# First block's second product from whole float32 words; w_out split in two afterwards

## The chip, the cores and the metric

The kernel runs on one core of one Trainium2 chip. The metric is the device time of one execution in microseconds (us). The kernel before takes 892.45 us (median of 3 runs, 891.19 to 892.52).

## What is computed

Three layers follow one another on 3072 tokens (4 sequences of 768) of width 384: a gated linear attention with decay (8 heads of 48), a dense gated feed-forward layer, and a mixture of 8 experts of which one is taken for each token. The change lies in the second layer:

```python
def _moe_ref(x, w_gate, w_val, w_out, rms_g):
    rms = np.sqrt(np.mean(x * x, axis=-1, keepdims=True) + 1e-06)
    xn = x / rms * rms_g
    g = xn @ w_gate
    silu = g * (1.0 / (1.0 + np.exp(-g)))
    val = xn @ w_val
    return (silu * val @ w_out).astype(np.float32)
```

`w_gate` and `w_val` are 384 x 1536, `w_out` is 1536 x 384. The experts' routing logits (16 columns) are linear in this layer's output, so the kernel appends `w_out @ w_gates` to `w_out` as 16 further columns: the second product is 400 wide.

## The kernel before, in words

**Number format.** The weights of the second layer arrive in HBM as float64. `decode` turns a piece of them into float32 on the chip: a DMA brings 64-bit words into `raw`, ScalarE scales the low words (L113), VectorE shifts and merges the high words (L114, L118), GpSimd adds both (L122) into a float32 tile `dt`. TensorE's one-pass format `fp32r` holds fewer bits than float32, so every operand is kept as two fp32r parts, high and low: ScalarE writes the high part (L125) and VectorE the rest by subtraction (L129). A product of two such operands is three matmuls: high by high, high by low, low by high (`mm3`, and L547 to L549 for the second product).

**Blocks.** The second layer runs over eight blocks of 384 tokens (`for j in range(NB)`), each over twelve slices f of the hidden width. `l1(f)` forms the two first products into two PSUM banks `a` (18 fp32r matmuls each 384 wide for both), ScalarE applies silu to the first (L531), VectorE multiplies by the second (L533), giving `sil`; ScalarE makes its high part `hh` (L535) and VectorE its low part `hl` (L538). `l2(f)`, two slices later, multiplies the 3 x 128 token columns of `hh` and `hl` as stationary operand by the two parts `wo[f // 2]` of `w_out`, adding into three PSUM banks `l` over all f (nine matmuls, 400 wide). At the end of a block ScalarE copies the banks to `xr` (L906).

**The first block** carries more work than the others. The 18 pieces of weights (for every two f two pieces of `w_gate` and `w_val` and one of `w_out`) are decoded while it runs: `decode_step` starts a piece's stages and finishes those of earlier pieces, six steps ahead of the block (`START`), the rest at every second `slot()` inside it. `route_columns` forms the 16 further columns for each f: TensorE transposes the decoded `w_out` rows (L505), ScalarE copies them to `wt` (L509), three small float32 matmuls follow (L513), and the result is split into the parts in `wo` (L516, L517). And in the slots of every block the attention of the next block's three tiles is computed, with float32 matmuls on TensorE (L408, L414, L431, L444, L450, L466), products on VectorE and GpSimd, a row norm `ss` (ACT L458, POOL L459 and L460), the scaling of `y` (ACT L480), its transposition (PE L484) and the two parts `xh`, `xl` (ACT L488, DVE L491).

**Order.** Each engine runs its instructions in the order in which the code is written (`tc.manual_schedule`), so a late instruction holds up all that stand behind it on the same engine. Tiles rotate in pools: `dt` has three buffers, the ring has 12 small and 6 big slots, and `wo` takes big ones.

Of the kernel before, what the change touches and what calls it, by code (L numbers as in the profile page):

```python
# [9 lines left out]
F32 = mybir.dt.float32  # L10
FR = mybir.dt.float32r
BF16 = mybir.dt.bfloat16
I32 = mybir.dt.int32
U32 = mybir.dt.uint32
AF = mybir.ActivationFunctionType
ALU = mybir.AluOpType
# [6 lines left out]
def kernel(  # L23
# [20 lines left out]
    nc = tc.nc  # L44
    B, S, _, H, D = rkv.shape
    N, DM = out.shape
    DFF = w_gate.shape[1]
    E, _, F2 = w1.shape
    P = 128
# [3 lines left out]
    KD = DM // P  # L53
    KF = DFF // P
# [4 lines left out]
    WIDTH = DM + 2 * E  # L59
# [17 lines left out]
    ring = ctx.enter_context(tc.tile_pool(name="ring", bufs=12))  # L77
# [20 lines left out]
    def words(src):  # L98
        return src.bitcast(U32) if src.dtype != U32 else src

    def decode(n, loads, dst, more=None):

        raw = loaded(n)
        for put, words_in in loads:
            nc.sync.dma_start(out=put(raw), in_=words_in)
        yield  # L110
        t = dec.tile([P, 2, DM], U32, tag="dt", bufs=3, name="dt")
        ti, tf, low = t.bitcast(I32), t.bitcast(F32), raw.bitcast(I32)[:, :, :, 0]
        nc.scalar.activation(out=low, in_=raw[:, :, :, 0], func=AF.Copy, scale=2.0 ** -29)  # L113
        nc.vector.tensor_scalar(  # L114
            t, raw[:, :, :, 1], 3, 0x3FFFFFF8, op0=ALU.logical_shift_left, op1=ALU.bitwise_and
        )
        yield
        nc.vector.scalar_tensor_tensor(  # L118
            out=t, in0=raw[:, :, :, 1], scalar=0xC0000000, in1=t, op0=ALU.bitwise_and,
            op1=ALU.bitwise_or,  # L120
        )
        nc.gpsimd.tensor_tensor(out=ti, in0=ti, in1=low, op=ALU.add)  # L122
        yield
        hi, lo = dst()
        nc.scalar.activation(out=hi, in_=tf, func=AF.Copy)  # L125
        if more:
            more(tf)
        yield
        nc.vector.tensor_tensor(out=lo, in0=tf, in1=hi.bitcast(F32), op=ALU.subtract)  # L129
        yield  # L130

    def split(raw, dst):
        nc.scalar.activation(out=dst[:, 0], in_=raw, func=AF.Copy)
        nc.vector.tensor_tensor(out=dst[:, 1], in0=raw, in1=dst[:, 0].bitcast(F32), op=ALU.subtract)
# [33 lines left out]
    def ring_view(shape, dtype=F32, big=None):  # L168
        n = 1
        for x in shape:  # L170
            n *= x
        t = slot_of(n, dtype, "rv", big)
        names = "abc"[:len(shape)]
        dims = " ".join(names)
        return t.rearrange(f"p ({dims}) -> p {dims}", **dict(zip(names[1:], shape[1:])))
# [87 lines left out]
    p1 = ph1.enter_context(tc.tile_pool(name="p1", bufs=1))  # L263
# [232 lines left out]

    gv = {}
    wo = {}
    routed = {}

    def route_columns(f, tf):

        o = bank("m", 3, [P, KD, P])
        for kk in range(KD):
            nc.tensor.transpose(o[:, kk], tf[:, kk * P:(kk + 1) * P], c["ident"])  # L505

        wt = turned[:, f % 4] if f < KF - 2 else dec.tile([P, 2, DM], F32, tag="dt", bufs=3, name="wt")[:, 0]
        wt = wt.rearrange("p (c f) -> p c f", c=KD)
        nc.scalar.activation(out=wt, in_=o, func=AF.Copy)  # L509
        yield  # L510
        o = bank("m", 3, [P, 2 * E])
        for kk in range(KD):
            nc.tensor.matmul(o, wt[:, kk], c["wr"][:, kk], start=kk == 0, stop=kk == KD - 1)  # L513
        t = wo[f // 2]
        hi, lo = t[:, 0, f % 2, DM:WIDTH], t[:, 1, f % 2, DM:WIDTH]
        nc.scalar.activation(out=hi, in_=o, func=AF.Copy)  # L516
        nc.vector.tensor_tensor(out=lo, in0=o, in1=hi.bitcast(F32), op=ALU.subtract)  # L517
        yield

    def l1(f, xh, xl, n, sub):  # L520
        t = gv[f]
        pg = []
        for a in range(2):
            o = bank("a", 2, [P, n])
            for kk in range(KD):
                mm3(o, t[:, 0, a, kk], t[:, 1, a, kk], xh[:, kk, 0:n], xl[:, kk, 0:n],
                    kk == 0, kk == KD - 1)
            pg.append(o)
            if a == 0:
                sil = p2.tile([P, n], F32, tag="sil", name="sil")  # L530
                nc.scalar.activation(out=sil, in_=o, func=AF.Silu)  # L531
                sub()
        nc.vector.tensor_tensor(out=sil, in0=pg[1], in1=sil, op=ALU.mult)  # L533
        hh = p3.tile([P, n], FR, tag="hh", name="hh")
        nc.scalar.activation(out=hh, in_=sil, func=AF.Copy)  # L535
        sub()
        hl = p3.tile([P, n], FR, tag="hl", name="hl")
        nc.vector.tensor_tensor(out=hl, in0=sil, in1=hh.bitcast(F32), op=ALU.subtract)  # L538
        return hh, hl

    def l2(f, h, acc):
        hh, hl = h
        t = wo[f // 2]
        wh, wl = t[:, 0, f % 2], t[:, 1, f % 2]
        for j, o in enumerate(acc):
            sl = slice(j * P, (j + 1) * P)
            nc.tensor.matmul(o, hh[:, sl], wh, start=f == 0, stop=False)  # L547
            nc.tensor.matmul(o, hh[:, sl], wl, start=False, stop=False)  # L548
            nc.tensor.matmul(o, hl[:, sl], wh, start=False, stop=f == KF - 1)  # L549
# [98 lines left out]
    def exhaust(g):  # L648
        for _ in g:
            pass  # L650

    with tc.manual_schedule():
# [34 lines left out]
        for f in range(KF):  # L687
            def dst(f=f):
                gv[f] = ring.tile([P, 2, 2, KD, P], FR, tag="ring", name="gv")
                return tuple(gv[f][:, s].rearrange("p a c f -> p a (c f)") for s in range(2))  # L690
            pieces.append(([
                (lambda t, a=a: t[:, a].rearrange("p (c f) t -> p c (f t)", c=KD),
                 src[:, 2 * f * P:2 * (f + 1) * P].rearrange("(c p) f -> p c f", p=P))
                for a, src in enumerate((words(w_gate), words(w_val)))
            ], dst))
            if f % 2:
                def dst(f=f):
                    wo[f // 2] = ring.tile(
                        [P, 2, 2, WIDTH], FR, tag="big", bufs=6, name="wo"
                    )  # L700
                    return tuple(wo[f // 2][:, s, :, 0:DM] for s in range(2))

                def more(tf, f=f):
                    for i in range(2):
                        routed[f - 1 + i] = route_columns(f - 1 + i, tf[:, i])

                pieces.append(([
                    (lambda t: t.rearrange("p a n t -> p a (n t)"),
                     words(w_out)[(f - 1) * P:(f + 1) * P, :].rearrange("(a p) n -> p a n", p=P))
                ], dst, more))  # L710
        gens_w = []
        done_w = [0]

# [32 lines left out]
        def decode_step():  # L746
            n = done_w[0]
            if n < len(pieces) + LAG:
                advance(n + 2, 1)
                advance(n, 2)  # L750
                if n >= LAG:
                    advance(n - LAG, 5)
                advance(n, 3)
                if n >= LAG - 1:
                    advance(n - LAG + 1, 4)
                done_w[0] += 1
            else:
                done_w[0] += 1
            routed_step()

        def weights_to(i):
# [72 lines left out]
        for j in range(NB):  # L834
# [24 lines left out]
            for f in range(KF + 2):  # L859
                if f < KF:  # L860
                    if j == 0:
                        weights_to(f + f // 2 + 1)
                    hs[f] = l1(f, xs[0], xs[1], n, slot)
                if f >= 2:
                    if f - 2 in routed:
                        exhaust(routed.pop(f - 2))
                    l2(f - 2, hs.pop(f - 2), acc)
                    slot()
                if j == NB - 1:
                    if f == 3:  # L870
                        lead = pick(c)
                        xw = expert_weights(0, lead)
                    if f >= 4:
                        next(xw, None)
                    if f == KF - 3:
                        xg0 = ring_view([EARLY // P, ROW])
                        nc.sync.dma_start(
                            out=xg0,
                            in_=scr.rearrange("(e a) c -> e a c", e=E)[ds(lead, 1), 0:EARLY, :]
                            .rearrange("o (t p) c -> p (o t) c", p=P),  # L880
                        )
                    if f == KF:
                        x0 = ring_view([2, KD, EARLY], FR)
                        transpose_in(c, xg0, EARLY, x0[:, 0], x0[:, 1])
                if j == 1 and ini < E:
                    init_rows(c, ini)
                    ini += 1
# [412 lines left out]
```

## Time and profile before

| what | value |
|---|---|
| median of 3 runs | 892.45 us |
| the profiled execution | 890.04 us |
| its span, first to last instruction | 888.3 us |
| TensorE busy (PE) | 853.3 us, 96% |
| VectorE busy (DVE) | 523.3 us, 59% |
| ScalarE busy (ACT) | 316.7 us, 36% |
| GpSimd busy (POOL) | 208.8 us, 24% |
| first block, first matmul to end | 44.05 to 152.3 us |
| second block, to its copy of the banks | 152.3 to 224 us |

The profiled execution is 1.7 us longer than its span and lies 2.4 us below the median of the runs. The records of the matmuls overlap, since a matmul's time from start to end is longer than the distance to the next one; the price of a matmul in a row of matmuls is therefore the distance between two starts, not its own length.

### The profile page before, as it was taken

The numbers are of one execution on the slowest core, as the hardware profiler recorded it, in microseconds if no ns is written. First come the engines' busy times: TensorE is split into PE (matmuls) and PEld (weight loads), VectorE is DVE, ScalarE is ACT, GpSimd is POOL, SyncE is SP. The second block draws the span as 40 slices with busy tenths as digits, with TensorE's granted clock in tenths as the row PEclk, the third lists the DMA queues.
The fourth block names the chain that finished last, engine by engine and source line by source line (L and its number), as shares of the span: only waits on it lengthen the run. The fifth ranks groups of instructions, "written<-read, shape, count | busy, mean of one in ns | idle before, by whom it ended". The sixth has DMA issues, their size and how long they took to land. (4 is left out here: it accounts for less than half of the span.)

```text
span 888.3 us, 15961 instructions
## 1 busy us (share of the span) xinstructions
PE 853.3 (96%) x6220; PEld 808.4 (91%) x6220; DVE 523.3 (59%) x1052; ACT 316.7 (36%) x667; POOL 208.8 (24%) x282
## 2 busy tenths in 40 slices
PE   7778989999999999999999999999999999999994
PEld 4577889999999999999999999999998999999994
DVE  8898854665565556465376366343556565565651
ACT  4655443232322322322323323223444434443531
POOL 6644431223131032032132132010011021122111
PEclk8889979999999999999999999999999999999998
DMA  8753421663221122042023020012164445445510
GB/s 231 207 178 107 134 89 48 165 170 117 73 63 55 46 81 55 12 122 55 10 82 80 29 81 20 1 53 83 58 199 150 132 148 153 145 124 176 167 40 22
DMA packets 63728, 87.98 MB, mean 99 GB/s; under 512 B 5538, under 2 KB 55220, under 8 KB 63652
## 3 DMA queue, kind: packets, MB, share of 16 engines
q1 hardware_dynamic: 60014, 77.36, 30.0%
q0 software_dynamic: 3312, 9.56, 2.9%
q8 instruction: 49, 0.80, 0.4%
q14 instruction: 27, 0.22, 0.1%
q10 hardware_dynamic: 326, 0.03, 0.0%
HBM read 70.71 MB, written 16.58 MB: 98 GB/s over the span
## 5 line engine op out<-in xcount | busy, mean ns | idle before, releaser
L164 PE MATMUL a<-xh,gv 128*128 128x384 f32 x1152 | 326.7, 349 | 1.6 <-ACT xh L488 1.5
L164 PEld LDWEIGHTS a<-xh,gv 128*128 128x128 f32 x1152 | 215.3, 193 | 4.8 <-ACT xh L488 1.6
L164 PE MATMUL a<-xl,gv 128*128 128x384 f32 x576 | 197.2, 342 | 0.2 <-DVE xl L491 0.2
L533 DVE TENSOR_TENSOR sil<-a,sil 128x384 f32<-128x384 f32 x96 | 53.3, 555 | 115.9 <-PE a L164 115.6
L164 PEld LDWEIGHTS a<-xl,gv 128*128 128x128 f32 x576 | 111.0, 193 | 0.6 <-DVE xl L491 0.6
L535 ACT ACTIVATE hh<-sil 128x384 fp32r<-128x384 f32 x96 | 50.5, 526 | 167.6 <-DVE sil L533 162.5
L531 ACT ACTIVATE sil<-a 128x384 f32<-128x384 f32 x96 | 47.3, 492 | 169.3 <-PE a L164 163.8
L164 PE MATMUL a<-xh,w1s 128*128 128x272 f32 (+7 forms) x384 | 106.1, 337 | 0.4 <-DVE hl L972 0.4
L547 PE MATMUL l<-wo,hh 128*128 128x400 f32 x288 | 102.3, 355 | 0.0
L548 PE MATMUL l<-wo,hh 128*128 128x400 f32 x288 | 99.6, 346 | 0.0
L549 PE MATMUL l<-wo,hl 128*128 128x400 f32 x288 | 98.9, 343 | 0.0
L240 POOL DMA_INDIRECT out_dram<-row,iu x30 | 35.4, 1181 | 196.3 <-DVE row L983 152.5
L164 PE MATMUL l<-hh,rows 128*128 128x272 f32 (+5 forms) x288 | 80.1, 342 | 0.0
L972 DVE SCALAR_TENSOR_TENSOR hl<-a,hh 128x256 fp32r<-128x256 f32 (+8 forms) x72 | 38.6, 539 | 67.5 <-ACT hh L971 67.4
L538 DVE TENSOR_TENSOR hl<-sil,hh 128x384 fp32r<-128x384 f32 x96 | 57.0, 594 | 35.6 <-ACT hh L535 35.6
L164 PEld LDWEIGHTS a<-xh,w1s 128*128 128x128 f32 x384 | 69.8, 188 | 1.6 <-DVE hl L972 0.6
L971 ACT ACTIVATE hh<-a 128x256 fp32r<-128x256 f32 (+8 forms) x72 | 34.6, 480 | 93.1 <-PE a L164 92.4
L164 PE MATMUL a<-xl,w1s 128*128 128x272 f32 (+7 forms) x192 | 64.5, 336 | 0.0
L398 POOL TENSOR_TENSOR y<-vt,g 128x384 f32<-128x384 f32 x23 | 22.4, 975 | 167.5 <-issue 62.6
L547 PEld LDWEIGHTS l<-wo,hh 128*128 128x128 f32 x288 | 54.3, 189 | 1.2
L549 PEld LDWEIGHTS l<-wo,hl 128*128 128x128 f32 x288 | 54.6, 190 | 0.2
L548 PEld LDWEIGHTS l<-wo,hh 128*128 128x128 f32 x288 | 54.2, 188 | 0.0
(235 smaller groups left out, 1394.1 us busy)
## 6 DMA issues: line engine op xcount, KB each, us to landing
raw<-in_moe_w_dram SPq DMA_DIRECT2D x64, 384.0 KB, 3.3
set<-in_feat_dram SPq DMA_DIRECT2D x46, 192.0 KB, 4.0
rk<-in_rkv_dram SPq DMA_DIRECT2D x18, 384.0 KB, 4.6
scr<-zrow SPq DMA_DIRECT2D x8, 788.0 KB, 6.2
set<-in_feat_dram SPq DMA_DIRECT2D x46, 96.0 KB, 2.4
vt<-in_rkv_dram SPq DMA_DIRECT2D x23, 192.0 KB, 2.4
raw<-in_moe_w_gate_dram SPq DMA_DIRECT2D x8, 384.0 KB, 3.8
raw<-in_moe_w_val_dram SPq DMA_DIRECT2D x8, 384.0 KB, 3.9
```

The costliest lines, as they stand in the source:

```text
L164: nc.tensor.matmul(o, a, b, start=start and i == 0, stop=stop and i == 2, skip_group_check=True)
L240: ins = nc.gpsimd.indirect_dma_start(out=dst, out_offset=bass.IndirectOffsetOnAxis(ap=idx, axis=0), in_=rows, in_offset=None, bounds_check ...
L398: nc.gpsimd.tensor_tensor(out=y, in0=vv, in1=g.unsqueeze(2).to_broadcast([P, H, D]), op=ALU.mult)
L531: nc.scalar.activation(out=sil, in_=o, func=AF.Silu)
L533: nc.vector.tensor_tensor(out=sil, in0=pg[1], in1=sil, op=ALU.mult)
L535: nc.scalar.activation(out=hh, in_=sil, func=AF.Copy)
L538: nc.vector.tensor_tensor(out=hl, in0=sil, in1=hh.bitcast(F32), op=ALU.subtract)
L547: nc.tensor.matmul(o, hh[:, sl], wh, start=f == 0, stop=False)
L548: nc.tensor.matmul(o, hh[:, sl], wl, start=False, stop=False)
L549: nc.tensor.matmul(o, hl[:, sl], wh, start=False, stop=f == KF - 1)
L971: nc.scalar.activation(out=hh, in_=o, func=AF.Relu)
L972: nc.vector.scalar_tensor_tensor(out=hl, in0=o, scalar=0.0, in1=hh.bitcast(F32), op0=ALU.max, op1=ALU.subtract)
```

## The change

In block 0 alone the second product is formed from float32 operands. `l1` ends with the product `h` as one float32 tile, without `hh` and `hl`; `l2_whole` runs one float32 matmul for each 128 tokens in place of three fp32r ones. `decode` leaves a piece of `w_out` as float32 in `whole_w`, two pieces in one big slot of the ring (the last in a tile of its own), and `route_columns` writes its 16 columns there whole. The two parts `wo` that the seven later blocks use are made by `split_wo`, once for each piece, from the whole words: in the `decode_step`s that come after the last piece, or when `l2` of block 1 needs them. `dt` has two buffers instead of three, and `wt` a tile in the pool where `hl` stands.

```diff
@@ def decode(n, loads, dst, whole=None):
-        t = dec.tile([P, 2, DM], U32, tag="dt", bufs=3, name="dt")
+        if whole:
+            t = whole().bitcast(U32)
+        else:
+            t = dec.tile([P, 2, DM], U32, tag="dt", bufs=2, name="dt")
...
+        if whole:
+            dst(tf)
+            yield
+            yield
+            return
         hi, lo = dst()
         nc.scalar.activation(out=hi, in_=tf, func=AF.Copy)
...
@@ def route_columns(f, tf):
-        wt = turned[:, f % 4] if f < KF - 2 else dec.tile([P, 2, DM], F32, tag="dt", bufs=3, name="wt")[:, 0]
+        wt = p3.tile([P, DM], F32, tag="hl", name="wt").rearrange("p (c f) -> p c f", c=KD)
...
-        nc.scalar.activation(out=hi, in_=o, func=AF.Copy)
-        nc.vector.tensor_tensor(out=lo, in0=o, in1=hi.bitcast(F32), op=ALU.subtract)
+        nc.scalar.activation(out=whole_w[f // 2][:, f % 2, DM:WIDTH], in_=o, func=AF.Copy)
+    def split_wo(k):
+        for f in (2 * k, 2 * k + 1):
+            if f in routed:
+                exhaust(routed.pop(f))
+        wo[k] = ring.tile([P, 2, 2, WIDTH], FR, tag="big", bufs=6, name="wo")
+        split(whole_w[k].rearrange("p a n -> p (a n)"), wo[k].rearrange("p s a n -> p s (a n)"))
@@ def l1(f, xh, xl, n, sub, whole=False):
+        if whole:
+            h = p3.tile([P, n], F32, tag="hh", name="h")
+            nc.vector.tensor_tensor(out=h, in0=pg[1], in1=sil, op=ALU.mult)
+            sub()
+            return h
+    def l2_whole(f, h, acc):
+        w = whole_w[f // 2][:, f % 2]
+        for j, o in enumerate(acc):
+            nc.tensor.matmul(
+                o, h[:, j * P:(j + 1) * P], w, start=f == 0, stop=f == KF - 1,
+                skip_group_check=True,
+            )
@@ def decode_step():
-            else:
-                done_w[0] += 1
+            elif len(wo) < KF // 2:
+                split_wo(len(wo))
+            done_w[0] += 1
@@ for j in range(NB): ... for f in range(KF + 2):
-                    hs[f] = l1(f, xs[0], xs[1], n, slot)
+                    hs[f] = l1(f, xs[0], xs[1], n, slot, j == 0)
...
-                    l2(f - 2, hs.pop(f - 2), acc)
+                    if j == 0:
+                        l2_whole(f - 2, hs.pop(f - 2), acc)
+                    else:
+                        while len(wo) <= (f - 2) // 2:
+                            split_wo(len(wo))
+                        l2(f - 2, hs.pop(f - 2), acc)
```

On ScalarE, in the middle of the first block, around the scaling of a tile's `y`, before:

```order
L113 ACTIVATE rv<-rv 128x768
L125 ACTIVATE gv<-dt 128x768
L516 ACTIVATE wo<-m 128x16
L535 ACTIVATE hh<-sil 128x384
L476 ACTIVATE states<-m 48x4x48 x2
L480 ACTIVATE y<-y,ss 128x384
L488 ACTIVATE xh<-m,g_col 128x128 x3
```

and of the change, at the same place (lines are six to eleven higher; `rv` in the third row is the slot with the whole words):

```order
L116 ACTIVATE rv<-rv 128x768
L133 ACTIVATE gv<-dt 128x768
L520 ACTIVATE rv<-m 128x16
L482 ACTIVATE states<-m 48x4x48 x2
L486 ACTIVATE y<-y,ss 128x384
L494 ACTIVATE xh<-m,g_col 128x128 x3
```

The instruction `hh`, which reads VectorE's `sil`, no longer stands ahead of `y`.

On VectorE, a little earlier in the program, from the preparation of `kq` to the addition that completes the same tile's `y` and the next piece, before:

```order
L376 RECIPROCAL front<-kq 128x4
L377 TENSOR_TENSOR kq<-set_81,kq 128x4x128
L114 TENSOR_SCALAR dt<-raw_673 128x768
L129 TENSOR_TENSOR wo<-dt,wo 128x2x384
L118 SCALAR_TENSOR_TENSOR dt<-raw_673,dt 128x768
L538 TENSOR_TENSOR hl<-sil,hh 128x384
L454 TENSOR_TENSOR y<-m,y 128x384
```

and of the change:

```order
L382 RECIPROCAL front<-kq 128x4
L383 TENSOR_TENSOR kq<-set_81,kq 128x4x128
L117 TENSOR_SCALAR dt<-raw_662 128x768
L121 SCALAR_TENSOR_TENSOR dt<-raw_662,dt 128x768
L460 TENSOR_TENSOR y<-m,y 128x384
```

The low parts of `w_out` and of `h` are gone from between them.

On VectorE at the end of the first block, around the last two products, before:

```order
L533 TENSOR_TENSOR sil<-a,sil 128x384
L472 TENSOR_TENSOR states<-m,states 48x4x48 x2
L538 TENSOR_TENSOR hl<-sil,hh 128x384
L491 SCALAR_TENSOR_TENSOR xl<-m,g_col,xh 128x128 x3
L517 TENSOR_TENSOR wo<-m,wo 128x16
L533 TENSOR_TENSOR sil<-a,sil 128x384
L538 TENSOR_TENSOR hl<-sil,hh 128x384
```

and of the change, with one row more ahead of them:

```order
L140 TENSOR_TENSOR wo<-rv,wo 128x800
L546 TENSOR_TENSOR h<-a,sil 128x384
L478 TENSOR_TENSOR states<-m,states 48x4x48 x2
L497 SCALAR_TENSOR_TENSOR xl<-m,g_col,xh 128x128 x3
L140 TENSOR_TENSOR wo<-rv,wo 128x800
L546 TENSOR_TENSOR h<-a,sil 128x384
L140 TENSOR_TENSOR wo<-rv,wo 128x800 x2
```

Four of the six splits stand here; the other two follow in the first slices of block 1. SyncE's and GpSimd's instructions keep their order.

## Rows read from the trace of the kernel before

**Rows 1.** Page, busy time, share of the span and instructions of an engine.

```profile
PE 853.3 (96%) x6220; PEld 808.4 (91%) x6220; DVE 523.3 (59%) x1052; ACT 316.7 (36%) x667; POOL 208.8 (24%) x282
```

**Rows 2.** Stretches: length; busy PE, PEld, DVE, ACT, POOL; granted clock; DMA share; GB/s.

```profile
44.00:121.00 77.00, 65.38 (x457) 61.79 (x458) 65.76 (x94) 39.40 (x80) 34.60 (x22) 0.88 0.45 141
121.00:152.30 31.30, 30.17 (x229) 28.68 (x228) 14.21 (x32) 8.89 (x23) 4.67 (x9) 0.91 0.10 27
152.30:224.00 71.70, 71.70 (x593) 68.42 (x592) 43.56 (x90) 21.04 (x49) 19.56 (x34) 1.00 0.53 151
```

**Rows 3.** Waits of TensorE in the first block: total us, times, longest.

```profile
PE m L484 <- ACT y L480: 5.6, 2, 3.7
PE m L505 <- POOL dt L122: 5.3, 3, 2.3
...
PE m L414 <- ACT wt L509: 1.1, 1, 1.1
PE m L431 <- DVE rq L387: 0.4, 1, 0.4
```

**Rows 4.** Same view as rows 2, three stretches at the lower clock.

```profile
85.70:92.50 6.80, 6.80 (x26) 6.80 (x27) 3.20 (x8) 3.37 (x8) 1.83 (x1) 0.50 0.00 1
...
116.50:123.20 6.70, 6.70 (x25) 6.70 (x24) 3.07 (x6) 3.09 (x7) 3.42 (x2) 0.50 0.27 106
...
130.10:133.40 3.30, 3.30 (x15) 2.86 (x15) 2.49 (x4) 0.02 (x1) 1.43 (x1) 0.50 0.69 179
```

**Rows 5.** Timeline of TensorE: start, length; nine matmuls of one l2, block 1.

```profile
201.06 0.34 PE L547 MATMUL l<-wo,hh 128*128 128x400 f32 x1
...
202.71 0.18 PE L557 MATMUL m<-acc,one_b 128*128 128x8 bf16 x1
```

**Rows 6.** Timeline of TensorE, float32 matmuls of the attention, 96 columns wide.

```profile
107.60 0.30 PE L444 MATMUL m<-states,rq 128*64 128x96 f32 x1
...
107.60 0.30 PE L444 MATMUL m<-states,rq 128*64 128x96 f32 x2
...
108.03 0.35 PE L444 MATMUL m<-states,rq 128*64 128x96 f32 x4
108.21 0.39 PE L450 MATMUL m<-vt,am 128*64 128x48 f32 x8
```

**Rows 7.** Groups on VectorE in the first block: busy us, mean ns, idle before.

```profile
L538 DVE TENSOR_TENSOR hl<-sil,hh 128x384 fp32r<-128x384 f32 x12 | 10.3, 859 | 3.6 <-ACT hh L535 3.6
...
L129 DVE TENSOR_TENSOR wo<-dt,wo 128x768 fp32r<-128x768 f32 x5 | 5.8, 1166 | 0.0
...
L517 DVE TENSOR_TENSOR wo<-m,wo 128x16 fp32r<-128x16 f32 x12 | 2.0, 167 | 5.8 <-ACT wo L516 5.8
```

**Rows 8.** The same of ScalarE.

```profile
L125 ACT ACTIVATE gv<-dt 128x768 fp32r<-128x768 f32 x9 | 7.6, 840 | 5.3 <-PE m L513 5.3
L535 ACT ACTIVATE hh<-sil 128x384 fp32r<-128x384 f32 x12 | 6.3, 525 | 24.8 <-DVE sil L533 24.8
```

**Rows 9.** Timelines, start and length: ACT, POOL and PE around the longest wait.

```profile
83.85 0.52 ACT L535 ACTIVATE hh<-sil 128x384 fp32r<-128x384 f32 x1 [1.75 <-DVE sil L533]
...
81.67 1.14 POOL L460 TENSOR_TENSOR ss<-ss,mhalf 128x1 f32<-128x1 f32 x1
...
85.62 0.88 PE L484 MATMUL m<-ident,y 128*128 128x128 f32 x3 [3.73 <-ACT y L480]
```

**Rows 10.** Timelines around waits for dt; then all hl (ns, min/median/max).

```profile
59.62 1.87 POOL L122 TENSOR_TENSOR dt<-dt,rv 128x768 int32<-128x768 int32 x1 [2.85 <-issue]
...
60.46 1.45 DVE L538 TENSOR_TENSOR hl<-sil,hh 128x384 fp32r<-128x384 f32 x1 [0.59 <-ACT hh L535]
...
61.53 0.85 ACT L125 ACTIVATE gv<-dt 128x768 fp32r<-128x768 f32 x1
...
105.56 0.55 PE L505 MATMUL m<-ident,dt 128*128 128x128 f32 x3 [1.10 <-POOL dt L122]
...
L538 DVE TENSOR_TENSOR hl<-sil,hh x96: 544/558/1734, 55.5 to 631.9; 128x384 fp32r<-128x384 f32 x96
```

More of the change, by code (lines that the diff above doesn't have):

```diff
@@ L99, in words, with decode @@
         return src.bitcast(U32) if src.dtype != U32 else src
-    def decode(n, loads, dst, more=None):
+    def decode(n, loads, dst, whole=None):
         raw = loaded(n)
@@ L123, in decode @@
         yield
+        if whole:
[3 more added lines that the diff above has]
+            return
         hi, lo = dst()
         nc.scalar.activation(out=hi, in_=tf, func=AF.Copy)
-        if more:
-            more(tf)
         yield
@@ L498 @@
     wo = {}
+    whole_w = {}
     routed = {}
@@ L505, in route_columns @@
             nc.tensor.transpose(o[:, kk], tf[:, kk * P:(kk + 1) * P], c["ident"])
-        wt = turned[:, f % 4] if f < KF - 2 else dec.tile([P, 2, DM], F32, tag="dt", bufs=3, name="wt")[:, 0]
-        wt = wt.rearrange("p (c f) -> p c f", c=KD)
+        wt = p3.tile([P, DM], F32, tag="hl", name="wt").rearrange("p (c f) -> p c f", c=KD)
         nc.scalar.activation(out=wt, in_=o, func=AF.Copy)
@@ L513, in route_columns, with l1 @@
             nc.tensor.matmul(o, wt[:, kk], c["wr"][:, kk], start=kk == 0, stop=kk == KD - 1)
-        t = wo[f // 2]
-        hi, lo = t[:, 0, f % 2, DM:WIDTH], t[:, 1, f % 2, DM:WIDTH]
-        nc.scalar.activation(out=hi, in_=o, func=AF.Copy)
-        nc.vector.tensor_tensor(out=lo, in0=o, in1=hi.bitcast(F32), op=ALU.subtract)
+        nc.scalar.activation(out=whole_w[f // 2][:, f % 2, DM:WIDTH], in_=o, func=AF.Copy)
         yield
-    def l1(f, xh, xl, n, sub):
+    def split_wo(k):
[4 more added lines that the diff above has]
+        split(whole_w[k].rearrange("p a n -> p (a n)"), wo[k].rearrange("p s a n -> p s (a n)"))
+    def l1(f, xh, xl, n, sub, whole=False):
         t = gv[f]
@@ L696, with whole @@
             if f % 2:
[L697 to L701, printed above, removed]
+                def whole(k=f // 2):
+                    if k == KF // 2 - 1:
+                        whole_w[k] = p1.tile([P, 2, WIDTH], F32, name="wlast")
+                    elif k % 2 == 0:
+                        pair = ring_view([2, 2, WIDTH], big=True)
+                        whole_w[k], whole_w[k + 1] = pair[:, 0], pair[:, 1]
+                    return whole_w[k][:, :, 0:DM]
                 def more(tf, f=f):
@@ L709 @@
                      words(w_out)[(f - 1) * P:(f + 1) * P, :].rearrange("(a p) n -> p a n", p=P))
-                ], dst, more))
+                ], more, whole))
         gens_w = []
@@ L755, in decode_step @@
                     advance(n - LAG + 1, 4)
-                done_w[0] += 1
-            else:
-                done_w[0] += 1
+            elif len(wo) < KF // 2:
+                split_wo(len(wo))
+            done_w[0] += 1
             routed_step()
```

## The prediction

> **What bounds the kernel now.** TensorE is busy for 96% of the span [rows 1], so the page alone says that only TensorE's work counts. The view by stretches says where that is not so [rows 2]. The second block takes 71.7 us at the full clock with TensorE busy throughout and VectorE at 43.6 us. The first block takes 108.3 us for the same products: 77.0 us while weights are decoded (44 to 121 us), with VectorE busy for 65.8, TensorE for 65.4 and a granted clock of 0.88, then 31.3 us in which VectorE is busy for 14.2 only. All that the change touches lies in these 108.3 us, apart from two splits in block 1. What it gains or loses there reaches the end unchanged, since the later blocks run TensorE without a break.
>
> Three views divide the first block's excess. TensorE's waits: 5.6 us for `y`, in two waits of 3.7 and 1.9; 5.3 us for the decoded `dt` that the routing columns need, in three of 2.3, 1.1 and so 1.9; 1.1 us for `wt` and 0.4 for `rq` [rows 3, 10]. The 1.9 us one for `dt` lies at the block's start, ahead of all that the change shortens, and is left alone below. The clock: stretches at 0.50, the lower of its two levels (1.2 GHz of 2.4), among them 85.7 to 92.5, 116.5 to 123.2 and 130.1 to 133.4 us [rows 4]. The first begins right behind the 3.7 us wait, which ends at 85.62 [rows 9], the others behind the 1.9 us wait for `y` and the one for `wt`. A stretch at half speed costs half its length: 3.4, 3.4 and 1.7 us. The rest is real work: routing columns, and three tiles of attention that every block has.
>
> **What is added: TensorE's work.** Nine fp32r matmuls of 400 columns go from 201.06 to 202.71 us, 0.184 us each, 0.55 us for the three that one float32 matmul replaces [rows 5]. No row shows a float32 matmul of this width. The nearest are the attention's, 96 columns wide [rows 6]. Two of them (four records, as each has two) take from 108.03 to 108.21, 0.18 us. If the two run one after the other, one costs 0.09 us, which is 0.375 us for 400 columns: the lower bound. If they run side by side, it is 0.75 us: the upper bound. Two records start at 107.60 and together fill the 0.30 us that one alone fills [rows 6], and they write different halves of the bank, so side by side is the likelier reading. I take 0.72, slightly under the bound, because part of a record's 0.09 us is its start. That is 0.17 us more for each of 36 matmuls: **+6.1 us** (bounds -6.3 and +7.2).
>
> The Trainium skill speaks against the change here: "FP8 and Floating Point Precision", section TensorE Precision Notes, says that true float32 makes four passes through the array. By that rule a matmul costs 4 x 0.184 = 0.74 us instead of 0.72, and the term is +6.6 us, not +6.1. The side-by-side reading of [rows 6] agrees with the rule; no row here shows it at this width.
>
> **What is removed.** VectorE loses `hl`, twelve times 0.86 us with 3.6 us of waiting for `hh`; the low parts of `w_out`, five times 1.17 us; and the routing columns' low parts, 2.0 us: 18.1 us of work [rows 7]. ScalarE loses `hh`, 6.3 us, ahead of which it stood idle for 24.8 us until VectorE's product came, and the high parts of `w_out` [rows 8]. Neither counts as such; it counts by what it takes off the waits:
>
> - The 3.7 us wait for `y`. ScalarE could scale `y` when its norm `ss` was there, at 81.67 + 1.14 = 82.8 us, but in its queue `hh` stood ahead, which started at 83.85 and waited for VectorE; `y` followed and TensorE went on at 85.62 [rows 9]. That is 2 us. Ahead of `ss` on VectorE stood a low part of `w_out` (1.17 us) and an `hl` (0.56 undisturbed) [rows 7, 10]; without them, with one decode step left in between, it comes 1 to 1.5 us earlier. TensorE arrives about when `y` is ready. Left: 0.5, **-3.2 us**.
> - The 1.9 us wait for `y`. One `hl` and one routing column, 0.7 us, stand on VectorE ahead of it, and TensorE comes later by a longer second product. **-0.9 us**.
> - The 2.3 us wait for `dt` at 66 us. An `hl` (at 60.46 us, 1.45 long behind a wait of 0.59) stood before the merge that `dt` needs [rows 10]. Without it ScalarE's high part at 61.53 [rows 10] is late next, so only about 1.1 of it goes. The 1.1 us one has `hl` and a low part of `w_out` ahead and nearly goes. **-2.0 us**.
> - The waits for `wt` and `rq`. ScalarE stood still for 5.3 us ahead of a high part of the gate weights until the last routing product that used the old `wt` buffers was done [rows 8]; `wt` now lies elsewhere. **-1.5 us**.
>
> Together **-7.6 us**, with TensorE's later arrival counted in. Of the clock I count the stretch behind the 3.7 us wait as gone, **-3.4 us**, and leave the two others; their bounds are nothing gone (0) and all three gone (-8.5).
>
> **What is moved at no cost.** Six splits at 0.88 us of ScalarE (0.840 x 800/768, [rows 8]) and about 1 to 1.2 of VectorE [rows 7]. Four stand in the stretch from 121 us, where VectorE is busy for 14.2 of 31.3 us and ScalarE for 8.9, two in block 1 with 28 us of VectorE free [rows 2]. Behind them on VectorE are the last products `h`, which are needed two slices later, and which free a bank that TensorE needs only after a second product and half a first one, eighteen matmuls at about 0.18 us, some 3 us later. Without this cover each would cost up to 1 us, 6 in all. Fewer `dt` buffers cost nothing: of any three successive pieces one is `w_out`, which no longer uses them. The big slots that `wo` takes over were read long before. Before the block, one low part leaves VectorE, but `xh` waits there for GpSimd and ScalarE: 0.
>
> **Sum.** 6.1 - 7.6 - 3.4 = -4.9 us. The profiled execution (890.04 us, span 888.3) becomes 885.1; it lay 2.4 us under the median, so on the median's scale **887.5 us**. With the side-by-side price from 0.70 to 0.75 (-0.7 to +1.1) and all or none of the stretches behind waits gone (-5.1 or +3.4) the forecast runs from -11 to about 0.
>
> **Rivals.**
>
> *The late chains stay late: slower.* VectorE and GpSimd get in each other's way: the `hl` at 60.46 took 1.45 us while GpSimd's addition ran from 59.62 to 61.49 [rows 10]; the median of all is 0.56. If the instruction that moves up takes over that delay, the waits end when they ended. The longer products in front of them are then swallowed by the waits, and the five products behind the last wait, that for `wt` before 130.1 us, remain: 5 x 3 x 0.17 = +2.6 us, **895.0 us**. It decides if `y` in the middle of the block is still scaled later than about 84.5 us. For it: 34.6 us of GpSimd in the 77 [rows 2]. Against it: at the longest wait it was the queue, not the speed, that held `y`. Chance 0.19.
>
> The Trainium skill, "GPSIMD Engine Reference", in its table of facts, has GpSimd's SBUF interfaces shared with VectorE for instructions with two SBUF inputs, as `hl` is; the trace agrees (1.45 us against 0.56). It bears out the mechanism, not that the next instruction suffers as much.
>
> *The clock gives nothing back.* The waits shrink, but a half-speed stretch of the same length stays, or starts elsewhere: -4.9 + 3.4 = -1.5 us, **891.0 us**, no change that can be told. For it: the first waits of the block remain. Chance 0.13.
>
> *Float32 is cheap.* At 0.375 us TensorE would save 6.3 us. But with less to do it waits for the same chains. Up to the last wait the time is then the forecast's, 7.6 + 3.4 less seven longer products at 0.51: -7.4 us. The five behind it give 5 x 3 x 0.18 = 2.7: -10.1 us, **882.4 us**; -17.3 if nothing but TensorE holds it. Chance 0.08.
>
> **Chances and range.** The forecast, from -11 to -2 us, has 0.60. Within 0.2% (1.8 us) is about what a measurement of this kernel can't tell from no change. Faster: forecast and cheap float32, 0.68; same 0.13; slower 0.19. The range reaches from a full return of the clock, 881.0, to the slower rival, 895.2; the forecast's own is 882 to 890.5.
>
> **What would show it.** 36 float32 products with 0.70 to 0.75 us between their starts (72 records); `y` in the middle scaled without an instruction ahead of it that waits for VectorE, at about 82 us; TensorE's waits in the first block near 6.5 us instead of 14; no half clock from 82 to 90 us; the block's copies at about 147.5 instead of 152.4 us, and later blocks of the old length. Wrong would be: the products near 0.37 us; waits as long as before; a split that TensorE waits for; half-speed stretches as long as before.

## The result, and the profile after

The changed kernel takes 880.6 us (median of 4 runs, 878.67 to 881.12); the kernel before, on the same chip, takes 891.82 us (4 runs, 890.98 to 892.52). The ratio is 0.9868, 95% interval 0.9851 to 0.9886: 11.8 us less by the ratio (the two medians are 11.2 apart), where 4.9 were forecast. The time lies 0.4 us below the range.

The page's line of busy times, of the kernel after:

```profile
PE 852.1 (97%) x6184; PEld 796.9 (91%) x6184; DVE 518.3 (59%) x1028; ACT 310.9 (35%) x655; POOL 207.0 (24%) x282
```

The profiled execution takes 880.62 us and its span is 878.9. TensorE is busy 1.2 us less than in [rows 1], VectorE 5 us less. The stretches of the first block up to its end, and the second block, columns as in [rows 2]:

```profile
44.00:121.00 77.00, 70.73 (x492) 61.16 (x491) 65.66 (x80) 37.44 (x77) 38.26 (x25) 0.96 0.47 145
121.00:143.50 22.50, 22.50 (x167) 17.14 (x166) 10.64 (x26) 7.78 (x17) 2.54 (x18) 1.00 0.16 51
143.50:215.00 71.50, 71.50 (x592) 68.24 (x591) 44.27 (x88) 22.13 (x50) 18.24 (x23) 1.00 0.51 144
```

The same 77 us hold more of TensorE's work (70.73 us busy, at a clock of 0.96 in place of 0.88), so less is left behind them: 22.5 us at the full clock instead of 31.3 at 0.91. The second block is as long as it was, 71.5 us, with the two splits in it. From its first matmul (45.88 us; 44.05 before) to its last copy the first block takes 97.7 us instead of 109.4, **-11.7 us**. TensorE's waits from 40 us to its end, which answer to [rows 3]:

```profile
PE m L512 <- POOL rv L125: 2.3, 2, 1.7
PE m L490 <- ACT y L486: 1.9, 2, 1.0
PE a L170 <- ACT xh L494: 1.6, 1, 1.6
PE m L512 <- POOL wlast L125: 0.8, 1, 0.8
PE a L170 <- DVE xl L497: 0.5, 1, 0.5
```

Line numbers are 6 to 31 higher here: L490 is `y`'s transposition, L512 that of the routing columns (its `rv` is the former `dt`), L560 the float32 product. The waits add up to 7.1 us. This view begins at 40 us, [rows 3] only at 44, so one wait for `y` ahead of the block's first matmul is in the one and not in the other. That wait, before and after, and two rows of before that [rows 3] leaves out:

```profile
40.90 0.55 PE L484 MATMUL m<-ident,y 128*128 128x128 f32 x3 [2.20 <-ACT y L480]
43.16 0.55 PE L490 MATMUL m<-ident,y 128*128 128x128 f32 x3 [0.88 <-ACT y L486]
PE a L164 <- ACT xh L488: 1.5, 1, 1.5
PE a L164 <- DVE xl L491: 0.2, 1, 0.2
```

From 40 us on, 16.3 us of waits became 7.1; from 44 us on, 14.1 became 6.2; and behind the block's first matmul, which the wait for `xh` precedes, 12.6 became 4.6. The longest wait for `y` was 3.73 us and is now 1.0 at most; those for `wt` and `rq` are gone. The same view of clock and busy time, around the first block's remaining half-speed stretches:

```profile
46.80:50.20 3.40, 3.40 (x12) 3.40 (x13) 3.40 (x6) 2.87 (x6) 0.79 (x2) 0.50 1.04 349
53.60:57.00 3.40, 3.40 (x13) 3.40 (x12) 3.40 (x4) 0.00 (x0) 1.12 (x2) 0.50 0.68 219
57.00:142.00 85.00, 82.47 (x616) 68.58 (x615) 63.75 (x86) 37.38 (x79) 33.14 (x28) 1.00 0.36 109
```

From 57 us on the granted clock is 1.00. All three late stretches of [rows 4], 17.0 us from edge to edge, are gone, not just the one that was counted. TensorE was busy throughout in them, so they cost half their length, 8.5 us. The timeline of TensorE around one second product (start, length):

```profile
63.04 2.18 PE L560 MATMUL l<-rv,h 128*128 128x400 f32 x6
65.06 0.74 PE L519 MATMUL m<-wr,wt 128*128 128x16 f32 x6
```

Three float32 matmuls (six records) take 2.02 us to the next start, 0.67 us each, against 1.65 us for the nine of [rows 5]. Twelve slices make **+4.4 us**. And the timelines of POOL, ACT, DVE and PE in the middle of the block, where the longest wait of [rows 9] stood:

```profile
77.85 1.88 POOL L125 TENSOR_TENSOR dt<-dt,raw 128x768 int32<-128x768 int32 x1 [1.04 <-issue]
78.02 2.13 DVE L117 TENSOR_SCALAR rv<-rv 128x768 uint32<-128x768 uint32 x1
80.28 1.15 POOL L466 TENSOR_TENSOR ss<-ss,mhalf 128x1 f32<-128x1 f32 x1
81.46 0.61 ACT L486 ACTIVATE y<-y,ss 128x384 f32<-128x384 f32 x1 [0.24 <-POOL ss L466]
82.13 0.55 PE L490 MATMUL m<-ident,y 128*128 128x128 f32 x3
84.42 0.55 DVE L117 TENSOR_SCALAR dt<-raw 128x768 uint32<-128x768 uint32 x1
```

`y` is scaled at 81.46 us, as soon as `ss` is there, and TensorE, which arrives later by its longer product, transposes it at 82.13 without a wait. A piece's shift at 78.02 still takes 2.13 us beside GpSimd's addition (0.55 alone, at 84.42), but nothing that `y` needs stands behind it.

### The profile page after: what moved, and what is told of

Same layout as the page of the kernel before. It is cut to its first block, busy times and chain, and to the rows that moved or that the text cites. A ratio compares the mean times of both kernels' runs of the same rounds, so it can differ in the third digit from the quotient of the medians.

```text
span 878.9 us, 15847 instructions
## 1 busy us (share of the span) xinstructions
PE 852.1 (97%) x6184; PEld 796.9 (91%) x6184; DVE 518.3 (59%) x1028; ACT 310.9 (35%) x655; POOL 207.0 (24%) x282
## 5 line engine op out<-in xcount | busy, mean ns | idle before, releaser
L170 PEld LDWEIGHTS a<-xh,gv 128*128 128x128 f32 x1152 | 212.1, 189 | 5.3 <-ACT xh L494 1.7
L549 DVE TENSOR_TENSOR sil<-a,sil 128x384 f32<-128x384 f32 x84 | 46.6, 555 | 107.1 <-PE a L170 105.9
L551 ACT ACTIVATE hh<-sil 128x384 fp32r<-128x384 f32 x84 | 44.0, 524 | 144.0 <-DVE sil L549 142.3
L571 PE MATMUL l<-wo,hh 128*128 128x400 f32 x252 | 88.6, 352 | 0.0
L572 PE MATMUL l<-wo,hh 128*128 128x400 f32 x252 | 86.6, 344 | 0.0
L573 PE MATMUL l<-wo,hl 128*128 128x400 f32 x252 | 86.2, 342 | 0.0
L554 DVE TENSOR_TENSOR hl<-sil,hh 128x384 fp32r<-128x384 f32 x84 | 46.7, 556 | 31.9 <-ACT hh L551 31.9
L170 PEld LDWEIGHTS l<-hh,rows 128*128 128x128 f32 x288 | 52.2, 188 | 1.2
L170 PE MATMUL l<-hl,rows 128*128 128x272 f32 (+5 forms) x144 | 48.5, 337 | 0.3 <-DVE hl L1003 0.3
L571 PEld LDWEIGHTS l<-wo,hh 128*128 128x128 f32 x252 | 47.3, 188 | 1.0
```

The costliest lines, as they stand in the source:

```text
L170: nc.tensor.matmul(o, a, b, start=start and i == 0, stop=stop and i == 2, skip_group_check=True)
```

## The experiments

The gain came out larger than forecast: either the shorter waits are worth more than was counted, or the clock is. The first four runs undo the moves one by one and together; the others change TensorE's work alone. Each expectation says what its theories are. Ratios are to the kernel before on the same chip, with 95% intervals; "against the changed kernel" compares two ratios, on 893 us. The waits given with a run count from 40 us on, so the one ahead of the block's first matmul is among them.

**The column copies back in their old place.**

```diff
-        wt = p3.tile([P, DM], F32, tag="hl", name="wt").rearrange("p (c f) -> p c f", c=KD)
+        wt = turned[:, f % 4] if f < KF - 2 else p3.tile([P, DM], F32, tag="hl", name="wt")
+        wt = wt.rearrange("p (c f) -> p c f", c=KD)
```

> The changed kernel with the routing columns' copies wt back in the old buffers for the first ten slices, so that the last gate weights' high part must again wait for the last routing product. Theory A (what counts is that hh, hl and the parts of w_out left VectorE's and ScalarE's queues): ScalarE stands still for some 5 us once more, where VectorE has little to do; 880.6 us plus 0 to 1.5. Theory B (the move of wt is what ended the waits and the falls of the clock): plus 5 or more, 885.6 us or above.

Measured 881.24 us, ratio 0.9876 (0.9856 to 0.9896): 0.7 us against the changed kernel, less than can be told. The new place of `wt` isn't the cause. Nor did it end the waits for `wt` and `rq`: with the old place back, this run's trace has neither.

**Cast and subtraction of h in the queues again**, their results unread:

```diff
             nc.vector.tensor_tensor(out=h, in0=pg[1], in1=sil, op=ALU.mult)
+            nc.scalar.activation(out=sil, in_=h, func=AF.Copy)
             sub()
+            nc.vector.tensor_tensor(out=sil, in0=h, in1=sil, op=ALU.subtract)
             return h
```

> The changed kernel with hh on ScalarE and hl on VectorE made again at their old places in the first block, into a buffer that no product reads; the products stay float32. Theory A: the scaling of y stands behind hh again, TensorE waits 2 to 4 us for it, and the clock falls behind that wait: plus 4 to 8, 884.6 to 888.6 us. Theory C (the float32 products keep TensorE busy, and that alone holds the clock): plus 0 to 1.

Measured 887.39 us, ratio 0.9944 (0.9924 to 0.9964): 6.8 us of the gain are lost. The two largest rows of TensorE's waits:

```profile
PE m L490 <- ACT y L486: 5.4, 3, 2.0
PE m L512 <- POOL rv L125: 2.5, 3, 1.5
```

Behind the block's first matmul the waits for `y` are 3.6 us in two, against 1.0 in the changed kernel and 5.6 before; the third of the row, 1.8 us, lies ahead of it. But no late stretch of the clock is lost with them; from 58.5 us to the block's end:

```profile
58.50:148.00 89.50, 83.74 (x620) 69.34 (x620) 68.41 (x96) 42.89 (x91) 31.87 (x24) 1.00 0.33 102
```

So waits return without late half-speed stretches. The forecast had tied the two together, and so had Theory A, whose time came true. In the profiled execution 4.4 of the 6.8 us lie in the first block: 2.8 us more of waits behind its first matmul, and some 1.7 because the half-speed stretch at its start was longer than in the changed kernel's first profile.

**Parts of the first three pieces of w_out at the old place**, in `decode`:

```diff
+            k = n // 3
+            if k < 3:
+                wo[k] = ring.tile([P, 2, 2, WIDTH], FR, tag="big", bufs=6, name="wo")
+                nc.scalar.activation(out=wo[k][:, 0, :, 0:DM], in_=tf, func=AF.Copy)
             dst(tf)
             yield
+            if k < 3:
+                nc.vector.tensor_tensor(
+                    out=wo[k][:, 1, :, 0:DM], in0=tf, in1=wo[k][:, 0, :, 0:DM].bitcast(F32),
+                    op=ALU.subtract,
+                )
             yield
             return
```

> The changed kernel with the parts of the first three pieces of w_out made where they were before, in the decoding, the other three late. Theory A: two low parts of about 1.2 us come back on VectorE at about 58 and 76 us: plus 1 to 3, 881.6 to 883.6 us. Theory C: no change, 880.6 within 0.5.

(`split_wo` then leaves these pieces out.) Measured 883.77 us, ratio 0.9904 (0.9882 to 0.9926): 3.2 us against the changed kernel, slightly more than Theory A's 1 to 3. The waits for `y` behind the block's first matmul are 1.7 us in two (one more, of 2.2, lies ahead of it), and there is no half-speed stretch behind 58.7 us:

```profile
58.70:146.00 87.30, 83.31 (x618) 69.00 (x617) 64.26 (x96) 37.03 (x84) 34.07 (x39) 1.00 0.35 111
```

**All three together.**

> The three of these together: the changed kernel with nearly all that had left the queues put back, only the product still in float32. Theory A: the waits and the half-speed stretches are back, and TensorE's longer products come on top: plus 9 to 15, 889.6 to 895.6 us. Theory C: at most plus 3, 883.6 us.

Measured 889.81 us, ratio 0.9964 (0.9945 to 0.9983). The three moves together are worth 8.6 us, a little less than their single effects (10.7). What is left of the change, the float32 product above all, though it has more work for TensorE than the three fp32r ones, is not slower but 3.2 us faster than before. TensorE waits 6.2 us for `y` from 40 us on (7.8 before), 4.4 of them behind the block's first matmul (5.6 before). The waits for `y` are thus mostly back, the longest at 2.8 us, and yet only one late stretch of half speed remains of three:

```profile
90.10:93.60 3.50, 3.50 (x13) 3.49 (x12) 2.95 (x6) 1.59 (x4) 0.41 (x1) 0.51 0.00 0
```

**Matmuls that compute nothing, in the kernel before**, ahead of `y`'s transposes:

```diff
+        for _ in range({3: 20, 4: 10}.get(i, 0)):
+            nc.tensor.matmul(
+                xT, c["one_b"], c["one_b"].unsqueeze(1).to_broadcast([P, KD, P]), start=True,
+                stop=True,
+            )
```

> The kernel before, with matmuls that nobody needs (20 and 10 of 384 columns, about 3.3 and 1.7 us at the full clock) written into the bank that the transposes of y overwrite, so that TensorE works during the two waits for y of the first block (3.7 and 1.9 us). Theory D (the half-speed stretches from 85.7 and 116.5 us are the waits' consequence): both are gone, 3.4 us each, with the filling inside the waits: 891.8 minus 4 to 7, 885 to 888 us. Theory E (the clock falls for another reason): the stretches stay, and the time is 891.8 to 893.

Measured 887.15 us, ratio 0.9943 (0.9914 to 0.9972): some 5 us faster for 30 matmuls more. The places of [rows 4] in its trace, with one new stretch ahead of them:

```profile
70.50:77.30 6.80, 6.80 (x27) 6.43 (x25) 3.31 (x6) 1.36 (x4) 2.63 (x2) 0.50 0.35 94
85.70:92.50 6.80, 6.34 (x53) 4.55 (x52) 5.70 (x7) 3.97 (x10) 5.01 (x4) 1.00 0.43 145
116.40:123.20 6.80, 6.57 (x42) 5.50 (x41) 4.33 (x10) 4.60 (x12) 4.54 (x4) 1.00 0.56 202
130.10:133.50 3.40, 3.40 (x32) 3.15 (x32) 3.37 (x6) 1.06 (x3) 1.37 (x1) 1.00 0.50 134
```

The three late stretches are at full clock. The one at 70.5 us, behind a wait for `dt` of 2.3 us that was not filled, may not be in every execution: this one took 890.72 us, 3.6 above the median.

**Less work for TensorE**, ten of the 36 float32 products left out of the changed kernel:

```diff
         for j, o in enumerate(acc):
+            if j == 2 and 0 < f < KF - 1:
+                continue
```

> The changed kernel without the products of the third 128 tokens for slices 1 to 10 of the first block (10 of 36 float32 products are left out, 0.67 us each). If TensorE's own work now sets the first block's time: minus 5.5 to 6.7, 874 to 875 us. If the chains of the other engines do: minus 1 to 3, 877.6 to 879.6 us.

Measured 882.86 us, ratio 0.9885 (0.9823 to 0.9947). 6.7 us of work less would be a ratio of 0.979; that is outside the interval, and the median is not even below the changed kernel's. The median misses both expectations; the interval rules out the first, but reaches into the second (a ratio of about 0.983 to 0.986). The waits grow from 7.1 to 10.7 us, 0.9 of it ahead of the block's first matmul, and two stretches at half speed appear that the changed kernel hasn't:

```profile
PE m L490 <- ACT y L486: 4.8, 3, 1.8
PE m L512 <- POOL rv L125: 2.9, 3, 1.5
PE a L170 <- ACT xh L494: 1.4, 1, 1.4
PE m L512 <- POOL wlast L125: 1.4, 1, 1.4
PE a L170 <- DVE xl L497: 0.2, 1, 0.2
```

```profile
85.90:89.30 3.40, 3.40 (x13) 3.40 (x12) 2.44 (x4) 0.91 (x4) 0.82 (x1) 0.50 0.00 0
120.00:123.40 3.40, 3.40 (x15) 3.30 (x14) 2.13 (x4) 1.09 (x3) 0.00 (x0) 0.50 0.20 58
```

**The same, with matmuls that compute nothing in place of the ten**, four of 384 columns for each:

```diff
             if j == 2 and 0 < f < KF - 1:
+                fill(o[:, 0:KD * P].rearrange("p (a f) -> p a f", a=KD), 4)
                 continue
```

> The changed kernel without the products of the third 128 tokens for slices 1 to 10 (so the output is incomplete), and in the place of each four bf16 matmuls of 384 columns that compute nothing (0.64 us, as long as what they stand for). If leaving the products out cost time because TensorE stood idle and its clock fell, the time comes back to the changed kernel's or below, ratio 0.984 to 0.988, without the half-speed stretches at 85.9 and 120.0 us; if it was something else, it stays where it was, ratio 0.987 to 0.991, with them.

Measured 881.34 us, ratio 0.9856 (0.983 to 0.9881), the changed kernel's. The same two stretches:

```profile
85.90:89.30 3.40, 3.40 (x19) 2.98 (x19) 2.35 (x4) 1.33 (x3) 1.85 (x1) 1.00 0.00 0
120.00:123.40 3.40, 3.40 (x31) 3.03 (x31) 0.98 (x2) 0.19 (x2) 0.83 (x1) 1.00 0.46 116
```

What TensorE computes doesn't matter there; with something to do in these places it stays at the full clock. In time the two kernels can't be told apart (their intervals overlap), so the traces carry this.

**The product alone made longer, in the kernel before**, by a fourth fp32r pass in the first block:

```diff
             nc.tensor.matmul(o, hh[:, sl], wl, start=False, stop=False)
+            if four:
+                nc.tensor.matmul(o, hl[:, sl], wl, start=False, stop=False)
...
-                    l2(f - 2, hs.pop(f - 2), acc)
+                    l2(f - 2, hs.pop(f - 2), acc, j == 0)
```

> The kernel before with one thing added: in the first block the second product takes a fourth fp32r pass (low part of h by low part of w_out), 36 matmuls of 0.184 us, so TensorE gets 6.6 us more work there and every other engine's queue stays as it was. Theory A (TensorE's work adds to the time of the block, and the changed kernel's gain is the other engines' relief alone): slower than before by 4 to 7 us, ratio 1.0045 to 1.008, with the same half-speed stretches. Theory D (in the first block TensorE's work falls into waits that are there anyway, and work in them keeps its clock from falling): at most 2 us slower, perhaps faster by up to 3 us, ratio 0.997 to 1.002, with waits that are shorter by some 4 to 6 us than before and fewer half-speed stretches behind 60 us.

Measured 892.41 us beside 894.11 us, ratio 0.9974 (0.9955 to 0.9994): not slower but some 2.3 us faster, with every other queue as before. At the places of [rows 4]:

```profile
85.70:92.50 6.80, 6.21 (x32) 6.18 (x33) 3.86 (x8) 3.88 (x9) 1.80 (x2) 0.75 0.05 18
116.40:123.20 6.80, 6.06 (x41) 5.96 (x40) 3.33 (x8) 3.06 (x8) 2.88 (x2) 1.00 0.15 60
130.10:133.50 3.40, 3.40 (x23) 3.15 (x23) 1.75 (x3) 0.16 (x1) 0.00 (x0) 1.00 0.01 5
```

The only late stretch left goes from 87.0 to 90.4 us: 3.4 us of 17.0. That gives 6.8 us back for 6.6 us of work. Its waits from 40 us on:

```profile
PE m L484 <- ACT y L480: 6.2, 3, 2.6
PE m L505 <- POOL dt L122: 4.0, 4, 1.6
PE a L164 <- ACT xh L488: 2.0, 1, 2.0
PE a L164 <- DVE xl L491: 0.2, 1, 0.2
PE m L414 <- ACT wt L509: 0.2, 1, 0.2
```

They add up to 12.6 us, where the kernel before has 16.3. A wait for `y` of 2.2 us lies ahead of the block's first matmul in both; behind it `y` costs 4.0 us instead of 5.6, the longest wait 2.6 instead of 3.7, and all waits 8.4 instead of 12.6. So 4.2 of the 6.6 us of work fall into waits, as Theory D has it, and the clock's return comes on top. The half-speed stretch at the block's start is longer than in the kernel before and costs some 1.2 us more. In sum, 6.6 - 4.2 - 6.8 + 1.2 = -3.2 us; the block is 3.0 us shorter in the traces.

This profiled execution was the fastest of its twelve (888.80 us, the median is 892.41), but the mean granted clock, which is on record for every run, says the same of the others. (1 - clock) x span is an estimate of what the lower level costs, TensorE's idle time included. Its median is 27.6 us in the 17 runs of the kernel before that were measured beside this one, and 20.5 in the 12 runs with the fourth pass: 7.1 us given back.

**Work in the early waits of the changed kernel**, 24 matmuls that compute nothing (`fill(o, n)` issues n of them):

```diff
@@ route_columns, y's transposes, l1
+        if f == 2:
+            fill(o, 9)
...
+        if i == 2:
+            fill(xT, 5)
...
+            if whole and f == 0 and a == 0:
+                fill(o.rearrange("p (a f) -> p a f", a=KD), 10)
```

> The changed kernel with 24 bf16 matmuls of 384 columns that compute nothing needed, put where TensorE waits early in the first block (9 ahead of the routing of the third slice, 10 ahead of the first product of the first slice, 5 ahead of y's transposes of the third tile); some 4 us of work. Theory D (half-speed stretches follow from TensorE's waits): the two stretches of 3.4 us at 46.8 and 53.6 us go or shrink, and the time falls by 1 to 3.4 us against the changed kernel, ratio to the kernel before 0.983 to 0.986. Theory A (work adds): the time rises by 2 to 4 us, ratio 0.989 to 0.992.

**The changed kernel again**, on the same chip, measured beside it:

> The changed kernel once more, unedited, beside the other two on the same chip: ratio 0.985 to 0.9886 by either theory, with no half-speed stretch between the first block's first 15 us and the last stage.

Measured 882.75 us for the changed kernel (881.33 to 884.08), ratio 0.9862 (0.9836 to 0.9888), and 880.18 us with the fills (878.56 to 881.2), ratio 0.9826 (0.9797 to 0.9856): 2.6 us less, with no run in common though the intervals touch. The early stretch and the rest of the block, first with the fills, then without:

```profile
43.80:57.00 13.20, 10.62 (x63) 8.53 (x62) 11.75 (x16) 7.82 (x15) 7.08 (x4) 1.00 0.61 196
57.00:142.00 85.00, 81.46 (x609) 67.25 (x608) 63.61 (x88) 37.00 (x78) 32.94 (x37) 1.00 0.37 112
```

```profile
43.80:57.00 13.20, 10.20 (x34) 9.69 (x35) 11.65 (x16) 6.46 (x13) 7.11 (x4) 0.51 0.61 196
57.00:142.00 85.00, 82.49 (x618) 68.66 (x617) 62.34 (x87) 37.58 (x79) 32.63 (x28) 1.00 0.35 109
```

The clock in the early stretch is 1.00 instead of 0.51. This is the fastest version, faster than both kernels. The early stretches also differ between executions of one kernel: 6.8 us in the first profile of the changed kernel, 13.6 in this one.

**All moves undone, with fills**: those of the last edit, and 12 ahead of the fourth tile's transposes.

> The kernel with all three moves undone (cast and subtraction of h, parts of the first three pieces of w_out, old place of the column copies; ratio 0.9964 to the kernel before) and with the fill matmuls of the edit before, plus 12 ahead of y's transposes of the fourth tile, where it waits 2.85 us: some 6 us of work that computes nothing. It separates the relief of the queues from the clock. If the moves paid only through the clock, this comes down to the changed kernel's time, ratio 0.984 to 0.988, with no half-speed stretch between 60 us and the last stage; if they paid as chains that end sooner, it stays above, ratio 0.990 to 0.995; if fills only add, 0.999 to 1.004.

Measured 887.51 us, ratio 0.9926 (0.9898 to 0.9953), 3.4 us below the same kernel without fills and 8.9 above the changed kernel with them. So the moves did not pay through the clock alone. In its trace a half-speed stretch stands at 70.0 us (0.53 to 77.2), behind waits for `rv` of 1.8 us and for `h` of 1.4 in two, but that execution took 891.04 us, the longest of its six, so it doesn't show what the median is made of.

## Why the prediction was wrong

**Product, priced 0.72 us: mis-sized.** It is 0.67 us, so +4.4 instead of +6.1 (1.7 us of the miss). The side-by-side reading of [rows 6] was right. "FP8 and Floating Point Precision" of the Trainium skill, section TensorE Precision Notes, has four passes for true float32. Four of this case's fp32r matmuls would by that be 0.74 us, an estimate. The trace bears out the order but comes out lower: a quarter of 0.67 us is 0.167 us, less than an fp32r matmul of its own at 0.184.

**Waits, -7.6: right.** Behind the block's first matmul 12.6 us became 4.6, which is -8.0. `y` fell from 5.6 to 1.0 us, and nothing stood ahead of its scaling on ScalarE that waited for VectorE; the waits for decoded words fell from 5.3 to 3.2 us, near the 2.0 forecast. The chains named were the ones: the queue work of `h` and that of `w_out`'s parts cost most when put back (6.8 and 3.2 us). The 1.5 us given to `wt` and `rq` came, but not by the move of `wt`: with its old place back these waits stay gone, at a cost of 0.7 us at most.

**The clock, "I count the stretch behind the 3.7 us wait as gone, -3.4 us, and leave the two others": this is the step that failed.** All three went, -8.5 us, 5.1 of the miss of 6.9. The forecast knew this as a bound but let the stretches hang on single waits. The runs showed something else: the longer product itself, priced as a loss, removes most of them. With longer products alone, in the kernel before, 17.0 us at half speed became 3.4 (the fourth pass), while the work filled 4.2 us of waits. With all three moves undone and only the float32 product left, 17.0 became 3.5. With the work of `h` alone put back there was none, though waits of 2.0 and 1.6 us for `y` were back. With ten products left out two returned, and with filling they went. The forecast took the product's length and the clock as two terms, where one pays for the other.

The length of a single wait doesn't decide where the clock falls. Two waits in the run with ten products left out:

```profile
111.32 0.55 PE L490 MATMUL m<-ident,y 128*128 128x128 f32 x3 [1.79 <-ACT y L486]
119.07 0.55 PE L512 MATMUL m<-ident,wlast 128*128 128x128 f32 x3 [1.43 <-POOL wlast L125]
```

Behind the first the clock stays at 1.00; behind the second, shorter one the stretch from 120.0 us begins. What does decide it is not shown.

**The sum.** 4.4 - 8.0 - 8.5 = -12.1 us, against -11.7 in the trace of the block and -11.8 by the ratio; the terms are 0.4 us too large together, which is not traced further. The clock of all runs agrees: by the estimate used for the fourth pass, the changed kernel's six runs lose 19.4 us where the 17 of the kernel before, measured beside them, lose 27.6, so 8.2 come back. The profiled executions differ by only 9.4 us, for the changed kernel's block starts 1.8 us later, at 45.88 us; the eleven other profiles start it between 44.73 and 47.54, so here the execution profiled before was early, not the one after late. The range's lower end stood for a full return of the clock: with the forecast's waits that is -10.0 us at 0.72 us a product and -10.7 at 0.70, a little above the 881.0 stated. At the measured 0.67 it is -11.7, or 880.8 us: the price took the result out of the range.

**Moves at no cost: right.** No wait of TensorE in the first two blocks is for a split, and block 1 takes 71.5 us as before.

**Rivals.** The late chains did not stay late: `y` is scaled at 81.46, not after 84.5, although a neighbour of GpSimd's addition was as slow as feared (2.13 us). The clock gave back all three late stretches, not nothing. Float32 is not at 0.375 us; and the run with fewer products shows that a cheaper one would have gained little, since TensorE would then wait for the same chains, at a lower clock.

**Left open.** The kernel before has one profile, so where its half-speed stretches lie in other executions is not shown. That it has them is: the profiled execution has a mean clock of 0.975, and the 55 later runs have medians of 0.969 to 0.971. How the 8.6 us of the moves divide into waits and clock can only be estimated. By the same estimate the kernel with all moves undone loses 20.9 us to the clock, and the one with only `wt` moved back, on the same chip, 18.9: some 2 us are clock and the rest is not. The kernel before loses 25.8 there, so about 5 us of the clock's return come with the product alone. The estimate also counts 10 to 15 us outside the first block, which vary from one profile to the next, so a difference of 2 us is at the edge of what it can tell.

## What to carry to other kernels

In a stage where TensorE waits for others, work put on it is not a cost to be added: price it by what it fills, and ask what the granted clock does behind each wait. Before a term for TensorE and a term for its clock are summed, test them together, with a run that adds or takes away TensorE's work alone. And where engines run in written order, look for the instruction that only waits for another engine ahead of something that a third one needs; here the cast and subtraction of `h` cost 6.8 us when put back.

## What was not expected of the hardware

- A float32 matmul of 400 columns takes 0.67 us in a row of such, less than four fp32r ones of the same width (0.74).
- 36 additional matmuls (6.6 us) made the kernel before 2.3 us faster, and 30 or 24 that compute nothing made the kernel before 5 and the changed kernel 2.6 us faster; 6.7 us of work left out gained nothing that can be measured.
- At the first block's start the changed kernel ran at half speed for 6.8 us in one profiled execution and for 13.6 in another.
